# One ring of three PSUM banks for the first MoE's groups and the value products

## The chip, the cores and the metric

The kernel runs on one core of a Trainium2 chip. The core has TensorE (PE) for matmuls, VectorE (DVE), ScalarE (ACT) and GpSimd (POOL) for the rest, and a queue (SP) that here issues nearly all DMAs. A matmul writes into PSUM, of which the kernel has eight banks; ACT and DVE read a product out of its bank, and only then may the next product be written there. The metric is the device time of one execution in microseconds.

## The reference

Attention over 4 batches, 8 heads, 576 tokens and head width 64 with rotary positions, then two MoE-like layers over the 2304 tokens:

```python
q_rot, k_rot = (rotate(q), rotate(k))
scores = scale * np.matmul(q_rot, k_rot.transpose(0, 1, 3, 2))
attn = np.exp(scores - np.max(scores, axis=-1, keepdims=True))
attn = attn / (np.sum(attn, axis=-1, keepdims=True) + 1e-09)
x = np.matmul(attn, v)            # (tokens, 512) after the heads are joined
h = np.maximum(np.maximum(x @ w1, x @ w2), x @ w3)      # first MoE, 512 -> 768
x = h @ w_out                                           # 768 -> 512
h = x @ w_in                                            # second MoE, 512 -> 2048
out = (h * (1.0 / (1.0 + np.exp(-h)))) @ w_out          # 2048 -> 512
```

## The kernel before

Attention runs over 80 tiles. A tile is 128 rows (or 64) of one pair of heads in one batch. For each tile PE computes the scores (L430 to L440, into `s`, of which there is one buffer of three banks), DVE takes the row maximum (L450), ACT takes the exponentials of both heads (L457) and scales them (L469), and four DMAs move blocks of the result from `e` to `pt` (L508), where DVE transposes them (L530). When the two or three tiles of a part are there, `av` (L559) computes the value product into the bank `xp`: one matmul at L571, eight at L575, then a read by ACT (L578) and a second one by DVE (L579), which give the high and the low half of x.

The first MoE of the batches that are done is worked off between the tiles. Its unit is a group (`group`, L662): 12 matmuls for one of the three products of `up` (L680), or 18 for `down` (L708), each of 256 or 320 columns. Of an `up` triple ACT copies the first product out (L687) and DVE takes the running maximum with the second and with the third (L689), so the third can be read only after the second. Of `down` ACT scales the product into `y` (L713), which has two buffers, and a DMA on SP's queue stores it (L714).

`attention` is a generator that yields once for each tile; the loop behind it then takes as many groups as the tile's budget allows. From tile 26 on (`LOOSE`) `b_now[0]` is 1, and a tile's scores are issued behind the last group; the flag goes back to 0 when attention ends. The order that the code is written in is not the order in which the engines work: a scheduler orders each engine's instructions anew from the dependencies and its own estimate of times. Each engine then works strictly in that order.

During attention the eight banks are: three for `s`, two for `tr` (transposes), two for `m` (`ps_m`, the groups) and one for `xp` (`ps_x`, the value products). A `Ring` gives out its buffers in turn, in the order in which the code asks. Tiles are named here as in the built program, by the bank's tag and a running number: `m_4866` and `xp_4866` are the same product in a bank of `m` and in the bank of `xp`.

Of the kernel before, what the change touches and what calls it, by code (L numbers as in the profile page):

```python
# [7 lines left out]
F32 = mybir.dt.float32  # L8
# [9 lines left out]
P = 128  # L18
# [4 lines left out]
def fused_kernel(  # L23
# [52 lines left out]
    ps_m = Ring(ctx, "ps_m", 2, space=PSUM)  # L76
# [20 lines left out]
    ps_x = Ring(attn_pools, "ps_x", 1, space=PSUM)  # L97
# [12 lines left out]
    zscr = {nm: dram.tile([P, KC * (F2 // 512) * 512], F32, name="z" + nm) for nm in ("wi", "wo")}  # L110


    ps_am, b_now = [], [0]

    def max_bank():
        ring, tag = (ps_am[0], "m") if ps_am else (ps_t, "tr") if b_now[0] else (ps_m, "m")
# [256 lines left out]
    def moved(b):  # L373
        return b > 0
# [114 lines left out]
    def blocks(pt):  # L489

        w = pt.shape[2]
        f = pt.rearrange("p c w -> p (c w)")
        return f[:, 0:8 * w].rearrange("p (i c k) -> p i c k", c=8, k=32), f[:, 8 * w:9 * w]
# [65 lines left out]
    def av(b, hp, r):  # L559
        if hp == 0 and r == 0:  # L560
            x_t[b] = x_p[b % 2].tile([P, NP * S], F32, tag="x", name="x").bitcast(F16).rearrange("p (a x s) -> p a x s", a=NP, x=2)
        pt, vv = pt_t.pop((b, hp, r)), v_t[b, hp]
        o, n = PARTS[r][:2]
        v4 = vv[:, 0:4, :].rearrange("p a x -> p (a x)").rearrange("p (h c d) -> p h c d", h=2, c=4)
        xp = ps_x.tile([P, 512], F32, tag="xp", name="xp")
        if moved(b):
            main, mixed = blocks(pt)
            turned = lambda c, g: main[:, :, c + 4 * g, :]
        else:
            mixed, turned = pt[:, 4, :], lambda c, g: pt[:, c + 5 * g, :]  # L570
        nc.tensor.matmul(xp[:, 0:n], vv[:, 4, :], mixed, start=True, stop=False)  # L571
        for c in range(4):
            for g in range(2):
                r = slice(64 * g, 64 * g + 64)
                nc.tensor.matmul(xp[r, 0:n], v4[:, g, c, :], turned(c, g), start=False, stop=(c == 3))  # L575
        xh, xl = x_t[b][:, hp, 0, o:o + n], x_t[b][:, hp, 1, o:o + n]
        sv = sv_t[b][0]
        nc.scalar.activation(out=xh, in_=xp[:, 0:n], func=AF.Copy, scale=sv)  # L578
        nc.vector.scalar_tensor_tensor(  # L579
            out=xl, in0=xp[:, 0:n], scalar=sv, in1=xh, op0=ALU.mult, op1=ALU.subtract  # L580
        )
# [43 lines left out]
    def attention():  # L625

        back = lambda j, n: tiles[j - n] if n <= j < len(tiles) + n else None
        for j in range(len(tiles) + 5):
            b_now[0] = int(j > LOOSE)
            if j < len(tiles):  # L630
                with tc.issue_after(last["group"]) if j > LOOSE else nullcontext():
                    tile_scores(tiles[j])
                tile_max(tiles[j])
            for n in (3, 2):
                key = back(j, n)
                if key and moved(key[0]) and n == 3 - (key in LAST):
                    tile_flip(key)
            for a in av_at.pop(j, ()):
                av(*a)
            key = back(j, 1)  # L640
            if key:
                tile_norm(key)
                if moved(key[0]):
                    tile_move(key)
            key = back(j, 2)
            if key:
                (tile_last if moved(key[0]) else tile_turn)(key)
            for f, a in events.pop(j, ()):
                f(*a)
            yield  # L650
# [11 lines left out]
    def group(passes, n, ps=None, more=False):  # L662

        first = ps is None
        if first:
            wide_n[0] += 1
            ring, tag = (ps_g[0], "mg") if ps_g and wide_n[0] % 7 > 1 else (ps_m, "m")
            ps = ring.tile([P, 512], F32, tag=tag, name=tag)
        for i, (l, r) in enumerate(passes):
            x = nc.tensor.matmul(ps[:, 0:n], l, r, start=(first and i == 0), stop=(not more and i == len(passes) - 1))  # L670
        last["group"] = x.ins
        return ps

    def moe1(b, pools):
# [5 lines left out]
        def up(half, f):  # L680
            o, n = PARTS[half][:2]
            part = []

            def evac(e, ps):
                t = tmp_p.tile([P, n], F32, tag="t", name="t")
                if e == 0:
                    last["ma"] = nc.scalar.activation(out=t, in_=ps[:, 0:n], func=AF.Copy, scale=2.0 ** -22).ins  # L687
                else:
                    last["mv"] = nc.vector.scalar_tensor_tensor(  # L689
                        out=t, in0=ps[:, 0:n], scalar=2.0 ** -22, in1=part[-1], op0=ALU.mult, op1=ALU.max  # L690
                    ).ins
                part.append(t)
                if e == 2:
                    hh = h1[half, f] = h1_p.tile([P, 2, n], F16, tag="h1", name="h1")
                    nc.scalar.activation(out=hh[:, 0], in_=t, func=AF.Copy)
                    nc.vector.tensor_tensor(out=hh[:, 1], in0=t, in1=hh[:, 0], op=ALU.subtract)

            for e in range(3):
                passes = []
                for c in range(KC):  # L700
                    i, fo = (f // FG * KC2 + c // 2) * 3 + e, (c % 2 * FG + f % FG) * P
                    wh, wl = W1.h(i)[:, fo:fo + P], W1.l(i)[:, fo:fo + P]
                    passes += [(wh, x[:, c, 0, o:o + n]), (wh, x[:, c, 1, o:o + n]), (wl, x[:, c, 0, o:o + n])]
                yield half, n * len(passes), False
                ps = group(passes, n)
                evac(e, ps)

        def down(half):  # L708
            o, n = PARTS[half][:2]

            def evac(m, ps):
                ysb = pools[2].tile([P, n], F32, tag="y", name="y")
                last["ma"] = nc.scalar.activation(out=ysb, in_=ps[:, 0:n], func=AF.Copy, scale=cy_t[b]).ins  # L713
                nc.sync.dma_start(out=yscr[:, m, b * S + o:b * S + o + n], in_=ysb)  # L714

            open_ = []
            for m in range(KC):
                passes = []
                for f in range(NF1):
                    wh = WO1.h(f)[:, m * P:(m + 1) * P]  # L720
                    wl = WO1.l(f)[:, m * P:(m + 1) * P]
                    h = h1[half, f]
                    passes += [(wh, h[:, 0]), (wh, h[:, 1]), (wl, h[:, 0])]
                yield half, n * len(passes), True
                if ps_g and half:
                    k = len(passes) - 3
                    open_.append((m, passes[k:], group(passes[:k], n, more=True)))
                else:
                    evac(m, group(passes, n))
            for m, passes, ps in open_:  # L730
                evac(m, group(passes, n, ps))
# [573 lines left out]
    def moe_groups():  # L1305
# [9 lines left out]
    costs = {av: 5800, qk_turn: 2900}  # L1315
    pace = [13600 - 3650 - sum(costs[f] for f, _ in jobs) for jobs in (
        [(av, a) for a in av_at.get(j, ())] + [x for x in events.get(j, ()) if x[0] is qk_turn] for j in range(len(tiles) + 5)
    )]
    debt = 0
# [126 lines left out]
```

## Time and profile before

| | |
|---|---|
| three timed runs | 977.44, 971.39 and 971.1 us, median 971.39 |
| profiled execution | 973.05 us, of it 971.3 us span |
| PE busy | 902.0 us (93%) |
| DVE, ACT, POOL busy | 710.9 (73%), 603.9 (62%), 442.3 us (46%) |
| mean granted TensorE clock | 0.978 |

The span reaches from the first to the last instruction of the profiled execution. Busy shares are means over stages with different limits; the change works only while `b_now[0]` is 1, which is from about 200 to 550 us of the span.

### The profile page before, as it was taken

What the parts mean: (1) busy time and instruction counts of PE and PEld (TensorE: products, weight loads), DVE (VectorE), ACT (ScalarE), POOL (GpSimd) and SP (SyncE); (2) the same over time, 40 slices, a digit from 0 to 9 for tenths busy, and PEclk for the clock granted to TensorE, in tenths of its full rate; (3) what the DMA queues carried; (4) which work ended last, traced back from release to release, by engine and by line L of the source; (5) the groups of instructions that cost most, each with busy time, mean ns of one, the idle gap of its engine ahead of it and who ended that gap; (6) DMA issues with size and microseconds to landing.
All of it is one profiled execution on the core that took longest, in us unless ns stands there. A gap on an engine that the chain in (4) does not pass through costs nothing.

```text
span 971.3 us, 19058 instructions
## 1 busy us (share of the span) xinstructions
PE 902.0 (93%) x6802; PEld 667.4 (69%) x6802; DVE 710.9 (73%) x1295; ACT 603.9 (62%) x1381; POOL 442.3 (46%) x482
## 2 busy tenths in 40 slices
PE   2787898899999899999998999999998999999997
PEld 1454665566655566566654687788887888888886
DVE  6779888867789576898887667465787866856654
ACT  1987587757687666798877535363555545544442
POOL 6745584960325400421211047264486467365363
PEclk9788999999999999999999999999999999999999
DMA  6943034958888984899989763164553434324101
GB/s 153 295 135 108 17 109 125 185 108 187 196 184 192 202 153 87 229 237 244 264 234 208 175 206 126 51 210 130 162 167 99 134 122 136 123 91 136 61 1 44
DMA packets 185198, 146.29 MB, mean 151 GB/s; under 512 B 51216, under 2 KB 168720, under 8 KB 185104
## 3 DMA queue, kind: packets, MB, share of 16 engines
q1 hardware_dynamic: 183600, 144.36, 57.9%
q8 instruction: 54, 0.88, 0.4%
q10 hardware_dynamic: 1504, 0.72, 0.3%
q14 instruction: 40, 0.33, 0.1%
HBM read 90.51 MB, written 26.21 MB: 120 GB/s over the span
## 4 chain that ended last, share of the span: by engine, by line
PE 54%; DMA 10%; DVE 7%; ACT 6%; SPq 4%; issue 3%; POOL 2%; DVEq 0%; ACTq 0%; POOLq 0%
PE m L670 11%; PE m L1102 8%; PE mb L1102 6%; DMA pt<-e 4%; PE c L1165 4%; PE a L1165 4%; PE b L1165 4%; PE xp L575 3%; PE mg L670 3%; PE s L440 3%; ACT e L457 2%; PE d L1165 2%; SPq L508 2%; DMA w8s<-w8scr 2%; POOL gsum L1049 1%
## 5 line engine op out<-in xcount | busy, mean ns | idle before, releaser
L670 PEld LDWEIGHTS <-w 128*128 128x128 f16 x1632 | 160.3, 99 | 62.2 <-issue 18.1
L670 PE MATMUL m<-x,w 128*128 128x256 f16 (+1 forms) x1356 | 188.6, 289 | 10.7 <-DVE t L689 5.1
L1165 PEld LDWEIGHTS <-g 128*128 128x128 f16 x1485 | 145.2, 98 | 16.9
L1102 PEld LDWEIGHTS <-w8s 128*128 128x128 f16 x1344 | 131.0, 98 | 16.1 <-issue 0.9
L450 DVE TENSOR_REDUCE nb<-s 128x2 f32<-128x1152 f32 (+1 forms) x80 | 98.5, 1232 | 37.2 <-PE s L440 30.0
L457 ACT ACTIVATE e<-s,nb 128x576 f32<-128x576 f32 x144 | 105.1, 734 | 28.6 <-DVE nb L450 26.1
L469 ACT ACTIVATE e<-e,rec 128x576 f32<-128x576 f32 x144 | 104.0, 766 | 11.2 <-DVE rec L467 10.4
L366 POOL TENSOR_TENSOR w<-qk,sin_sb 128x512 f32<-128x512 f32 (+2 forms) x40 | 42.8, 1072 | 122.7 <-DMA qk<-in_q_dram 93.5
L575 PE MATMUL xp<-pt,vd 128*64 128x256 f32 (+1 forms) x512 | 79.0, 422 | 0.9 <-DVE pt L530 0.9
L440 PE MATMUL s<-T 64*128 64x512 f32 x256 | 78.7, 685 | 0.0
L970 POOL TENSOR_TENSOR zs<-za 128x128 f32<-128x128 f32 x32 | 16.5, 527 | 129.8 <-DMA za<-zwi 68.3
L530 DVE STREAM_TRANSPOSE pt<-pt 128x1024 f32<-128x1024 f32 (+1 forms) x60 | 67.6, 1127 | 9.4 <-DMA pt<-e 9.4
L1054 DVE SCALAR_TENSOR_TENSOR g<-gsum,sg,g 128x1024 f16<-128x1024 f32 x36 | 49.5, 1383 | 23.7 <-ACT g L1053 23.4
L1116 POOL TENSOR_TENSOR z<-t 128x256 f32<-128x256 f32 x32 | 27.1, 845 | 87.4 <-DVE t L1108 51.3
L1053 ACT ACTIVATE g<-gsum,sg 128x1024 f16<-128x1024 f32 x36 | 40.8, 1141 | 36.4 <-POOL gsum L1049 36.4
L670 PE MATMUL m<-h,wo 128*128 128x256 f16 (+1 forms) x448 | 62.1, 286 | 0.5 <-POOL wo L175 0.3
L575 PEld LDWEIGHTS xp<-pt,vd 128*64 128x64 f32 x512 | 35.6, 139 | 36.7 <-issue 15.7
L670 PEld LDWEIGHTS <-wo 128*128 128x128 f16 x512 | 49.5, 98 | 16.2 <-issue 2.5
L940 POOL TENSOR_TENSOR z<-z 128x256 f32<-128x256 f32 x32 | 29.6, 952 | 41.7 <-DMA z<-zwo 41.2
L1165 PE MATMUL b<-w,g 128*128 128x256 f16 x376 | 48.5, 273 | 0.0
L1165 PE MATMUL a<-w,g 128*128 128x256 f16 x376 | 47.9, 273 | 0.0
L1165 PE MATMUL c<-w,g 128*128 128x256 f16 x376 | 47.6, 273 | 0.0
(265 smaller groups left out, 1989.9 us busy)
## 6 DMA issues: line engine op xcount, KB each, us to landing
w8s<-w8scr SPq DMA_DIRECT2D x64, 448.0 KB, 4.2
pt<-e SPq DMA_DIRECT2D x192, 128.0 KB, 4.0
z<-in_moe_w_in_dram SPq DMA_DIRECT2D x32, 256.0 KB, 3.6
z<-in_moe_w_out_dram SPq DMA_DIRECT2D x32, 256.0 KB, 3.8
w8scr<-w8o SPq DMA_DIRECT2D x32, 256.0 KB, 3.7
w<-in_moe_w_dram SPq DMA_DIRECT2D x6, 768.0 KB, 5.2
wo<-in_moe_w_dram SPq DMA_DIRECT2D x6, 768.0 KB, 5.3
qk<-in_q_dram SPq DMA_DIRECT2D x32, 128.0 KB, 3.1
```

The lines of the kernel that those rows point to most:

```text
L366: tt(out=w4, in0=t4, in1=sin2, op=ALU.mult)
L440: last["s"] = last["score"] = nc.tensor.matmul(s[:, o:o + 512], qs[r], kt[r], start=True, stop=True).ins
L450: x = nc.vector.tensor_reduce(out=nb[:, 0:m], in_=both(s, 0, 960, 576) if m > 1 else s[:, 0:576], op=ALU.max, axis=AX.X, negate=True)
L457: x = nc.scalar.activation(out=e[:, HK[g]], in_=s[:, SK[g]], func=AF.Exp, bias=nb[:, g:g + 1], accum_out=sm[:, g:g + 1])
L469: nc.scalar.activation(out=e[:, HK[g]], in_=e[:, HK[g]], func=AF.Copy, scale=r[:, g:g + 1])
L530: nc.vector.transpose(out=x, in_=x)
L575: nc.tensor.matmul(xp[r, 0:n], v4[:, g, c, :], turned(c, g), start=False, stop=(c == 3))
L670: x = nc.tensor.matmul(ps[:, 0:n], l, r, start=(first and i == 0), stop=(not more and i == len(passes) - 1))
L1053: nc.scalar.activation(out=h, in_=x, func=AF.Copy, scale=sg_t[jb])
L1054: nc.vector.scalar_tensor_tensor(out=l, in0=x, scalar=sg_t[jb], in1=h, op0=ALU.mult, op1=ALU.subtract)
L1102: nc.tensor.matmul(o, l, r, start=(i == 0), stop=(i == len(passes) - 1))
L1165: x = nc.tensor.matmul(ps, l, r, start=first, stop=last_, skip_group_check=True)
```

## The change

A new helper, `product_bank`, counts the products. Two of three get the next buffer of `ps_m`, the third gets the buffer of `ps_x`. While `b_now[0]` is set, both the groups and the value products ask it for their bank; outside that stretch everything is as before. The number of banks, of matmuls, of reads and of DMAs stays the same.

```diff
-    ps_am, b_now = [], [0]
+    ps_am, b_now, third = [], [0], [0]
+
+    def product_bank():
+
+        third[0] += 1
+        ring, tag = (ps_m, "m") if third[0] % 3 else (ps_x, "xp")
+        return ring.tile([P, 512], F32, tag=tag, name=tag)
...
-        xp = ps_x.tile([P, 512], F32, tag="xp", name="xp")
+        xp = product_bank() if b_now[0] else ps_x.tile([P, 512], F32, tag="xp", name="xp")
...
-            ps = ring.tile([P, 512], F32, tag=tag, name=tag)
+            ps = product_bank() if b_now[0] else ring.tile([P, 512], F32, tag=tag, name=tag)
```

The scheduler makes another order of it. In the changed kernel lines from L119 on stand six further down, so that L670 is L676 there. The first place is on PE, between the scores of two neighbouring tiles, `s_4695` and `s_4783`. `4866`, `4960` and `5027` are groups of 12 matmuls of 256 columns, `tr` are transposes. Before:

```order
L440 MATMUL s_4695<-T_3480 128x512 x2
L475 MATMUL tr_4716<-ident_81,e_4529 128x128
L476 MATMUL tr_4716<-ident_81,e_4529 64x128
...
L670 MATMUL m_4960<-x_3716,w_0_141 128x256
...
L670 MATMUL m_5027<-x_3716,w1f_140 128x256
...
L430 MATMUL s_4783<-T_3480,qd_0_124 128x512
L431 MATMUL s_4783<-T_3480,qd_0_124 128x64
L519 MATMUL tr_4801<-ident_81,e_4639 128x128
```

Two whole groups, 24 matmuls, stood between the scores, and `4866` came ahead of them. At the same place of the changed kernel:

```order
L446 MATMUL s_4695<-T_3480 128x512 x2
L481 MATMUL tr_4716<-ident_81,e_4529 128x128
L482 MATMUL tr_4716<-ident_81,e_4529 64x128
...
L676 MATMUL xp_4866<-x_3716,w1f_140 128x256
...
L436 MATMUL s_4783<-T_3480,qd_0_124 128x512
L437 MATMUL s_4783<-T_3480,qd_0_124 128x64
L525 MATMUL tr_4801<-ident_81,e_4639 128x128
...
L676 MATMUL xp_4960<-x_3716,w_0_141 128x256
```

One group, `4866`, now stands between the scores, and `4960`, which takes the same bank, follows behind the second of them; `5027` comes later still.

The second place is SP's queue behind the four moves of `e_3549`. `y_3702` is the output of a `down` group on its way to memory; `pt<-e` are a tile's moves, `z`, `zwi` and `za` weights of the second MoE, `qk` and `vd` inputs. Before:

```order
L508 DMA pt_3571<-e_3549 32x8x128 x4
L854 DMA z_3_3757<-in_moe_w_in_dram 128x256
L829 DMA zwi_137<-z_3595 128x2x128
L308 DMA qk_4166<-in_q_dram 64x2x64
L305 DMA qk_4166<-in_k_dram 128x4x64
L508 DMA pt_3734<-e_3605 32x8x128 x3
L714 DMA yscr_135<-y_3702 128x256
```

Seven DMAs stood between those moves and the store. In the changed kernel:

```order
L514 DMA pt_3571<-e_3549 32x8x128 x4
L321 DMA vd_0_130<-in_v_dram 128x2x256
L970 DMA za_4338<-zwi_137 128x2x128
L720 DMA yscr_135<-y_3702 128x256
L860 DMA z_3_3757<-in_moe_w_in_dram 128x256
```

The store has moved up: two DMAs are now between them.

## Rows read from the trace of the kernel before

**Rows 1.** The page, engines: busy us, share of the span, instructions.

```profile
PE 902.0 (93%) x6802; PEld 667.4 (69%) x6802; DVE 710.9 (73%) x1295; ACT 603.9 (62%) x1381; POOL 442.3 (46%) x482
```

**Rows 2.** Windows: stretch, its length, busy time of each engine, PEclk, DMA share, GB/s.

```profile
200.00:550.00 350.00, 334.02 (x2219) 213.06 (x2216) 278.53 (x557) 266.68 (x739) 89.17 (x120) 0.99 0.86 195
```

**Rows 3.** PE's waits from 200 to 550 us: total us, times, longest us.

```profile
PE m L670 <- DVE t L689: 4.3, 3, 2.4
PE s L437 <- ACT e L457: 3.6, 6, 0.9
PE m L670 <- ACT y L713: 2.1, 1, 2.1
PE s L430 <- ACT e L457: 1.9, 3, 1.2
PE m L670 <- ACT t L687: 1.5, 1, 1.5
```

**Rows 4.** Timeline of PE: start us, us, instruction, [idle before <-releaser].

```profile
268.21 0.38 PE L670 MATMUL m<-x,w1f 128*128 128x256 f16 x2 [0.63 <-DVE t L689]
...
317.27 1.79 PE L670 MATMUL m<-x,w 128*128 128x320 f16 x12 [1.49 <-ACT t L687]
334.48 0.43 PE L670 MATMUL m<-x,w1f 128*128 128x320 f16 x2 [2.06 <-ACT y L713]
...
425.25 1.47 PE L670 MATMUL m<-x,w 128*128 128x256 f16 x12 [1.29 <-DVE t L689]
...
516.72 4.97 PE L670 MATMUL m<-x,w 128*128 128x320 f16 x24 [2.41 <-DVE t L689]
```

**Rows 5.** Timeline of ACT and DVE, the reads that those matmuls waited for.

```profile
316.78 0.44 ACT L687 ACTIVATE t<-m 128x320 f32<-128x320 f32 x1
...
333.95 0.47 ACT L713 ACTIVATE y<-m,cy 128x256 f32<-128x256 f32 x1 [3.35 <-DMA yscr<-y]
...
424.80 0.40 DVE L689 SCALAR_TENSOR_TENSOR t<-m,t 128x256 f32<-128x256 f32 x1
...
515.04 1.25 DVE L530 STREAM_TRANSPOSE pt<-pt 128x1024 f32<-128x1024 f32 x1 [3.36 <-DMA pt<-e]
516.21 0.45 DVE L689 SCALAR_TENSOR_TENSOR t<-m,t 128x320 f32<-128x320 f32 x1
```

**Rows 6.** Timeline of SP's queue around the store of y.

```profile
322.21 2.69 SPq L508 DMA_DIRECT2D pt<-e  x4
...
329.65 0.55 SPq L714 DMA_DIRECT2D yscr<-y  x1
```

**Rows 7.** Timeline, one tile's scores, its maximum, its second exponential, the next scores.

```profile
408.43 1.13 PE L440 MATMUL s<-T 64*128 64x512 f32 x4
...
409.75 1.34 DVE L450 TENSOR_REDUCE nb<-s 128x2 f32<-128x1152 f32 x1
...
412.04 0.72 ACT L457 ACTIVATE e<-s,nb 128x576 f32<-128x576 f32 x1
...
412.91 1.12 PE L430 MATMUL s<-T,qd 128*128 128x512 f32 x2 [0.36 <-ACT e L457]
```

**Rows 8.** Timeline, the end of `4866` (5 of these 17), its read by ACT.

```profile
405.90 2.02 PE L670 MATMUL m<-x,w 128*128 128x256 f16 x17
...
408.78 0.38 ACT L687 ACTIVATE t<-m 128x256 f32<-128x256 f32 x1
```

**Rows 9.** Windows behind two of the waits; PEclk is the third number from the end.

```profile
335.00:339.00 4.00, 4.00 (x22) 2.12 (x21) 0.17 (x1) 3.88 (x12) 3.76 (x4) 0.57 0.95 195
...
516.00:520.00 4.00, 3.28 (x13) 1.84 (x13) 3.87 (x10) 3.30 (x9) 0.00 (x0) 0.57 0.55 176
```

**Rows 10.** Groups of DVE, 200 to 550 us, and timeline of one value product.

```profile
L579 DVE SCALAR_TENSOR_TENSOR x<-xp,vs,x 128x256 f16<-128x256 f32 (+1 forms) x22 | 11.2, 510 | 12.0 <-ACT x L578 11.8
...
404.76 0.76 PE L575 MATMUL xp<-pt,vd 128*64 128x320 f32 x4
...
408.55 0.55 DVE L579 SCALAR_TENSOR_TENSOR x<-xp,vs,x 128x320 f16<-128x320 f32 x1
```

## The prediction

> **What bounds the kernel now.** I began with the page: PE is busy 93% of the span and no other engine over 73% [rows 1], so PE bounds it, and a change that adds no matmul can only give or take PE's idle time and its slow stretches. The table by stretches then narrows this to the only part that the change touches: from 200 to 550 us PE is busy 334.0 of 350 us [rows 2], so 16.0 us is idle there. PE's own waits in that stretch say for what [rows 3]. A product waits for a bank to be read out: 4.3 behind DVE, 2.1 and 1.5 behind ACT, together 7.9 us in five waits. The scores wait for the one score buffer: 3.6 + 1.9 = 5.5 us in nine waits. The rest is small. The timeline shows the five bank waits one by one: 0.63, 1.49, 2.06, 1.29 and 2.41 us [rows 4].
>
> Two of them cost more than their idle time. In the 4 us behind the waits of 2.06 and 2.41 us the granted clock is 0.57 on the mean [rows 9], so most of that time is at the lower of the two levels, 1.2 GHz instead of 2.4. What this costs is seen at 516.72: 24 matmuls took 4.97 us [rows 4]; at the pace of 317.27, where 12 took 1.79 us and so one follows the other after (1.79 - 0.30)/11 = 0.135 us, they would take 23 x 0.135 + 0.30 = 3.41. That is 1.5 us, and I take the same for the other stretch. All that the banks cost is 7.9 + 3.0 = 10.9 us, and this bounds what more freedom in banks can give.
>
> **Why those waits arise** decides what a third bank does for them [rows 5]. At 334.48 ACT's read began only at 333.95, because ACT had stood 3.35 us for a store of y. At 516.72 DVE's read began at 516.21, behind a transposition that had itself waited 3.36 us for its moves. At 425.25 the read at 424.80 was that of the third product of a triple that PE had worked ahead of the second; it had to wait for the second's maximum. Only at 317.27 had PE simply come too soon: 12 matmuls' end to the read at 316.78 is ordinary. So four of five come from a reader that is late, not from a bank that is asked for too often.
>
> **The change part by part.** It adds no instruction. A group's bank is now asked for again three products later, but the value products count among the three, and their bank is no longer their own. So I counted, for each product on PE's new order, the matmuls between the last of the bank's former holder and its own first, at 0.135 us for 320 columns and (2.02 - 0.27)/16 = 0.109 us for 256 [rows 4, 8].
>
> *The five waits.* At 317.27 the former holder is now a value product that is long done: -1.5, the whole. At 425.25 the predecessor is the second of its triple and no longer the third, which passes its bank to a later group: -1.3. At 268.21 the predecessor is the same, with 4.9 us of work between where there were 4.2: -0.6, the whole. At 516.72 it is also the same, with 4.3 us in place of 3.4: -0.9, and 1.5 us stay, with their slow stretch, as long as the transposition waits for its moves as it did. At 334.48 predecessor and work between are as before (4.0 us), so the third bank itself gives nothing. But the store of y that ACT waits for has moved up in SP's queue. Before, SP ended the four moves at 322.21 + 2.69 = 324.90 and came to the store at 329.65 [rows 6], seven DMAs and 4.75 us later, 0.68 us each. Now two stand between, 1.4 us, so that the store goes 3.4 us earlier and covers the 3.35 us: -2.1 and -1.5 for the clock. If one of those two DMAs waits for its buffer, this is 0. Together -7.9, between -1.5 (317.27 alone) and -10.9.
>
> *The scores.* From the end of one tile's scores to the next there must be time for the maximum and both exponentials: the scores that began at 408.43 ended at 409.56, the second exponential at 412.76, and PE went on at 412.91 [rows 7], so about 3.4 us. PE hides that with what stands in between. At this place that was 24 matmuls and two transposes, 2.9 us, and PE waited 0.36. Now 12 matmuls stand there, 12 x 0.109 + 0.3 = 1.6 us: the wait becomes 1.8. Over all 54 pairs of neighbouring tiles, before, 11 had less than 3.4 us between them and lacked 5.6 us in sum, where 5.5 was measured as the nine waits [rows 3]; now 15 have less and lack 10.7. I take the difference, +5.1, behind which stands the tile's whole chain. Ends: 0, if these waits fall into the same gaps as others, and +7, with one slow stretch more.
>
> *Other returns of a bank.* Six are now under 2.1 us of work, before two were in this stretch. The shortest is `4866` to `4960`: only one score and one transpose, 1.1 us, stand between. ACT read `4866` until 409.16, after it had ended at 405.90 + 4 x 0.109 + 0.27 = 406.6 [rows 8], 2.6 us; but the wait of 1.8 us for `s_4783` stands between the two, so it costs nearly nothing more. The other five have 1.6 to 2.1 us. I take +1.5 for all of them, between 0 and +6 (one microsecond each), near the low end since the one return that I could time is hidden.
>
> The waits of transposes for new q and k, and those of value products for their moved blocks, I leave at nothing: they hang on POOL and the DMAs, and PE works the value products later than before, not earlier.
>
> **Sum.** -7.9 + 5.1 + 1.5 = -1.3 us. The profiled execution of 973.05 would become 971.8; it lies 1.7 above the median of 971.39, from which I get **970.1 us**.
>
> **A rule against this count.** The five waits have shown a reader that is late [rows 5], and two banks that already turn. The Trainium skill, Perfetto Trace Analysis, in Matmuls under Optimizing Tensor Performance, says that independent groups should rotate through different banks so that the reading of one overlaps the next one's matmuls. By that rule one bank more in the turn takes all five waits away; the trace agrees with it at 317.27 alone. That is the first rival.
>
> **The rivals.** *Faster: the third bank covers all bank waits*, and the scores find their cover as before. For it: 7.9 us of 16.0 idle us are bank waits [rows 2, 3], and half of all products now have over 4.3 us between. Against it: the late readers and the thinner cover of the scores. It gives -10.9, 960.5 us. Chance 0.2.
>
> *Slower: the value product holds up the ring.* A value product is read twice, by ACT and then by DVE. The example ended at 404.76 + 0.76 = 405.52 and was free when DVE had done, at 409.10 [rows 10], 3.6 us later. Before, only the next value product, many microseconds later, needed that bank; now a group does, with 3.7 us of work between on the median and about 3 in the tenth part with the least. There are 22 such products in the stretch [rows 10]. While the second read comes within 3.6 us this costs nothing; it decides as soon as DVE comes later than 3.7. With half a microsecond for each, 22 x 0.5 = 11.0, and one more slow stretch of 1.5: 970.1 + 12.5 = 982.6 us. For it: DVE waited 11.8 us for ACT's half of that read [rows 10], and DVE has a maximum, a transposition and weights in its queue. Against it: most of these reads came sooner. Chance 0.22.
>
> *The banks were not what counted*: the waits go and come back elsewhere, 971.4. That lies inside the forecast, not beside it.
>
> **How the numbers follow.** A measurement of this kernel can tell about 1% from no change, 9.7 us. The forecast, within 1%, has 0.58; the faster rival 0.2, the slower one 0.22, and these are also the chances of the three outcomes. The least sum is -10.9 + 0 + 0, the greatest -1.5 + 7 + 6 = +11.5, so 960.5 to 982.9. Each rival sits at one of these ends with a fifth, and about half of each lies beyond: I take 960 to 983.
>
> **What would show it.** In the changed trace from 200 to 550 us: PE's bank waits some 3 us and no more than 5; none at 317, and the one behind the store of y gone, with the store close behind the four moves and a clock of 1.0 there; the scores' waits about 10 us, one of some 1.8 us ahead of `s_4783`. Idle time of PE near 15 us, and one slow stretch in place of two. I am wrong if the scheduler's new order makes a long wait that this count cannot see, since it takes the readers' delays as they were: a queue of DVE or ACT that now stands at another DMA moves a bank's return by 3 us and brings a slow stretch along.

## The result

The changed kernel takes 980.61 us (median of 10 runs, 977.09 to 985.47), the kernel before 975.06 us in the 10 runs beside it (969.34 to 978.0). The ratio is 1.0064 with an interval of 1.0040 to 1.0088. So the change costs 0.64%. That lies inside the forecast range, but the forecast was a small gain, and no change at all is ruled out by the interval. The profiled execution took 980.79 us (span 978.7 us), 7.7 us more than the profiled one before.

### The profile after

On the page PE does the same work as before [rows 1]: 902.3 us in 6802 matmuls. What has grown is the rest of the span.

```profile
PE 902.3 (92%) x6802; PEld 667.4 (68%) x6802; DVE 712.0 (73%) x1295; ACT 604.5 (62%) x1381; POOL 442.7 (45%) x482
```

The windows of the changed kernel say where: PE's idle time from 200 to 550 us rose from 16.0 us [rows 2] to 23.6. The last two rows are the 4 us behind the waits at 334 and 518 (PEclk third from the end).

```profile
200.00:550.00 350.00, 326.38 (x2169) 207.48 (x2167) 276.34 (x548) 262.85 (x729) 91.71 (x122) 0.99 0.87 192
...
334.50:338.50 4.00, 4.00 (x23) 2.15 (x23) 0.54 (x2) 4.00 (x13) 1.56 (x4) 0.64 1.09 245
...
518.00:522.00 4.00, 2.20 (x15) 1.36 (x14) 3.92 (x9) 3.62 (x11) 0.00 (x0) 1.00 0.51 131
```

PE's waits of the changed kernel from 200 to 560 us, in the columns of [rows 3]: the scores now wait 8.2 + 4.0 = 12.2 us (before 5.5), and the products wait for a bank 4.2 + 3.2 + 2.5 + 0.6 = 10.5 us (before 7.9). So in this profile the wait that the third bank was to shorten is longer, and the other has more than doubled. A second profile of each kernel, further down, has 8.5 us of bank waits for 9.3, and 12.6 us of scores' waits for 6.4: that the scores wait twice as long repeats, that the banks' waits rose does not.

```profile
PE s L436 <- ACT e L463: 8.2, 7, 2.0
PE m L676 <- ACT y L719: 4.2, 1, 4.2
PE s L443 <- ACT e L463: 4.0, 6, 1.3
PE m L676 <- DVE t L695: 3.2, 2, 2.3
PE xp L676 <- DVE x L585: 2.5, 2, 2.2
...
PE xp L577 <- DVE t L695: 0.6, 1, 0.6
```

The timeline of PE in the changed kernel shows the waits that answer to [rows 4], and the largest new ones. Those of 317 and 425 us are gone. The one at 334 is twice as long as before, the one at 518 is 0.88 us. Those at 540 and 553, and the scores' wait at 394, were not there. 414.63 is `s_4783`.

```profile
333.96 0.69 PE L676 MATMUL m<-x,w1f 128*128 128x320 f16 x2 [4.18 <-ACT y L719]
...
393.81 1.12 PE L436 MATMUL s<-T,qd 128*128 128x512 f32 x2 [2.02 <-ACT e L463]
...
414.63 1.13 PE L436 MATMUL s<-T,qd 128*128 128x512 f32 x2 [1.37 <-ACT e L463]
...
518.23 2.20 PE L676 MATMUL m<-x,w 128*128 128x320 f16 x15 [0.88 <-DVE t L695]
...
540.50 0.43 PE L676 MATMUL m<-h,wo1f 128*128 128x320 f16 x2 [2.27 <-DVE t L695]
...
552.89 0.43 PE L676 MATMUL xp<-h,wo1f 128*128 128x320 f16 x2 [2.20 <-DVE x L585]
```

The timeline of ACT and DVE shows the readers behind three of them, as [rows 5] did before. ACT was free at 326.51 and stood until the store of y had ended. At 540 and 553 DVE had stood at a transposition whose moves had not come, and read the product only afterwards. At 540 only 1 us of other work lies between the two. At 553 there is more: ACT stood 1.72 us for the store of a weight and came to its half of the read at 550.40, and DVE did 3 us of other work between the transposition and its own half. Behind the longest wait of the scores, at 394, stands a late maximum: DVE began it at 390.82, though those scores had ended at 387.84.

```profile
326.32 0.19 ACT L472 ACTIVATE rec<-sm 128x2 f32<-128x2 f32 x1
333.44 0.48 ACT L719 ACTIVATE y<-m,cy 128x256 f32<-128x256 f32 x1 [6.93 <-DMA yscr<-y]
...
390.82 1.35 DVE L456 TENSOR_REDUCE nb<-s 128x2 f32<-128x1152 f32 x1
...
537.71 1.25 DVE L536 STREAM_TRANSPOSE pt<-pt 128x1024 f32<-128x1024 f32 x1 [3.37 <-DMA pt<-e]
...
539.98 0.47 DVE L695 SCALAR_TENSOR_TENSOR t<-m,t 128x320 f32<-128x320 f32 x1
...
547.90 1.25 DVE L536 STREAM_TRANSPOSE pt<-pt 128x1024 f32<-128x1024 f32 x1 [2.45 <-DMA pt<-e]
549.67 0.72 ACT L950 ACTIVATE w8o<-zs,wihalf 128x512 f16<-128x512 f32 x1 [1.72 <-DMA w8scr<-w8o]
...
552.30 0.53 DVE L585 SCALAR_TENSOR_TENSOR x<-xp,vs,x 128x320 f16<-128x320 f32 x1
```

And SP's queue in the changed kernel, to be held against [rows 6]: only two DMAs stand between the moves and the store, as forecast, but the moves themselves have sunk from 322.21 to 325.65, and the store is issued at 329.64 as it was at 329.65. Between these moves and the four moves of the tile ahead of them, which start at 315.53 (314.71 before, second block), now stand ten DMAs in place of six.

```profile
315.53 3.86 SPq L514 DMA_DIRECT2D pt<-e  x4
...
325.65 2.69 SPq L514 DMA_DIRECT2D pt<-e  x4
328.39 0.61 SPq L321 DMA_DIRECT2D vd<-in_v_dram  x1
329.05 0.49 SPq L970 DMA_DIRECT2D za<-zwi  x1
329.64 0.41 SPq L720 DMA_DIRECT2D yscr<-y  x1
```

```profile
314.71 2.74 SPq L508 DMA_DIRECT2D pt<-e  x4
```

### The profile page after: what moved, and what is told of

Same layout as the page of the kernel before. It is cut to its first block, busy times and chain, and to the rows that moved or that the text cites. A ratio compares the mean times of both kernels' runs of the same rounds, so it can differ in the third digit from the quotient of the medians.

```text
span 978.7 us, 19036 instructions
## 1 busy us (share of the span) xinstructions
PE 902.3 (92%) x6802; PEld 667.4 (68%) x6802; DVE 712.0 (73%) x1295; ACT 604.5 (62%) x1381; POOL 442.7 (45%) x482
## 4 chain that ended last, share of the span: by engine, by line
PE 56%; DVE 10%; DMA 7%; ACT 5%; issue 3%; SPq 2%; POOL 2%; DVEq 0%; ACTq 0%; POOLq 0%
PE m L676 9%; PE m L1108 8%; PE mb L1108 6%; PE c L1171 4%; PE a L1171 4%; PE b L1171 4%; PE s L446 3%; DMA pt<-e 3%; PE mg L676 3%; PE xp L676 3%; PE d L1171 2%; PE xp L581 2%; PE m L581 2%; SPq L514 2%; DVE pt L536 2%
## 5 line engine op out<-in xcount | busy, mean ns | idle before, releaser
L676 PEld LDWEIGHTS <-w 128*128 128x128 f16 x1632 | 159.3, 99 | 59.6 <-issue 15.7
L676 PE MATMUL m<-x,w 128*128 128x256 f16 (+1 forms) x1040 | 146.3, 288 | 7.6 <-ACT t L693 3.1
L1122 POOL TENSOR_TENSOR z<-t 128x256 f32<-128x256 f32 x32 | 27.1, 847 | 88.8 <-DVE t L1114 53.9
L676 PEld LDWEIGHTS <-wo 128*128 128x128 f16 x512 | 49.5, 98 | 17.6 <-issue 3.8
L676 PE MATMUL m<-h,wo 128*128 128x256 f16 (+1 forms) x368 | 51.7, 286 | 0.8 <-DVE h L702 0.3
L581 PE MATMUL xp<-pt,vd 128*64 128x320 f32 (+1 forms) x320 | 47.3, 414 | 1.2 <-DVE pt L536 1.2
L373 POOL TENSOR_TENSOR qk<-qk,cos_sb 128x512 f32<-128x512 f32 (+2 forms) x44 | 46.3, 1056 | 2.8
```

The lines of the kernel that those rows point to most:

```text
L373: tt(out=t4, in0=t4, in1=cos2, op=ALU.mult)
```

## The experiments

In time order, in groups. Ratios are to the kernel before, run beside each. The quoted texts name theories by letters; what a letter stands for is said with each group.

**Which part of the stretch.** Theory A: the loss is made in the last tiles of attention, where the new waits of 2.27 and 2.20 us stand. Theory B: it is made earlier, by the new order. `shared[0]` takes the place of `b_now[0]` in the two calls of `product_bank`, and is set for a part of the tiles:

```diff
+            shared[0] = int(LOOSE < j < 75)
```

> The ring of three works only from tile 26 to 74; from tile 75 on groups and value products have their own banks again. PE's order is that of the changed kernel up to about 508 us. Theory A (the loss is made in the last tiles, where a down group waits for the third product of a triple and another for the second read of a value product, 2.3 and 2.2 us, and two scores for 0.8 and 0.7 us): the loss of 5 to 6 us goes, ratio to the kernel before 1.000, 0.997 to 1.003. Theory B (the loss is spread: the scores' thinner cover costs 6.7 us all over the stretch): 1.004 to 1.007, as the whole change.

Measured: 978.01 against 974.01 us, ratio 1.0038 (1.0019 to 1.0057).

The second has the ring only in the last tiles:

```diff
+            shared[0] = int(j >= 75)
```

> The complement: the ring of three only from tile 75 to the end of attention, own banks before. PE's order is that of the kernel before up to about 525 us. Theory A: nearly the whole loss, 4 to 7 us, ratio 1.004 to 1.007, with waits of over 2 us for a bank between 530 and 560 us. Theory B: at most a tenth of the stretch, so under 1 us, ratio 0.999 to 1.001.

Measured: 974.69 us, ratio 1.0017 (0.9994 to 1.0041); no bank wait above 2 us stands from 530 to 560 us. Theory A falls as the main cause: by the medians more than half of the loss is there without the last tiles. Theory B's figures are missed too: 1.0038 lies a little below its 1.004 to 1.007, and 1.0017 above its 0.999 to 1.001, so a part of the loss does belong to the last tiles.

**The value products keep their own bank**, and the groups take three in turn all the same, so that `xp` serves both in an order of its own:

```diff
-        xp = product_bank() if b_now[0] else ps_x.tile([P, 512], F32, tag="xp", name="xp")
+        xp = ps_x.tile([P, 512], F32, tag="xp", name="xp")
```

> Value products always take the bank xp; the groups alone take three banks in turn, so that every third group shares xp with the value products. Theory A: groups that wait for DVE's second read of a value product, and value products behind groups, stay, so no gain on the change: ratio 1.002 to 1.010. Theory B: the ring's length is what thins the scores' cover; with value products out of the count the order comes nearer to that of before: 0.999 to 1.004.

Measured: 995.82 us, ratio 1.0211 (1.0180 to 1.0242), far beyond what either theory gave. PE's waits from 190 to 575 us are those of groups for that one bank, 18.7 us in the three largest lines:

```profile
PE xp L676 <- DVE x L585: 8.8, 6, 3.8
PE xp L676 <- DVE t L695: 5.1, 2, 3.1
PE xp L676 <- ACT t L693: 4.8, 2, 4.4
```

The first line, 8.8 us, is the prediction's slower rival: a group waits for the second read of a value product. In the other two, 9.9 us, the group waits for the reads of another group in that bank. The changed kernel, where the value product takes its turn, keeps most of this away: 2.5 us behind L585.

**The store of y.** Theory C: the wait behind the store of y makes the loss. The store is issued by ACT, in the changed kernel and in the kernel before:

```diff
-                nc.sync.dma_start(out=yscr[:, m, b * S + o:b * S + o + n], in_=ysb)
+                nc.scalar.dma_start(out=yscr[:, m, b * S + o:b * S + o + n], in_=ysb)
```

> The changed kernel with the stores of y issued by ACT and not by SP. PE's order of groups and scores is nearly the changed kernel's: 15 pairs of scores with too little work between them, 10.7 us lacking, as there. Theory C (the 4.2 us wait at 334 us and its slow stretch come from SP's queue, which is issuing without a pause and comes to the store of y 7 us after ACT has written it): ACT's wait of 6.9 us for that store falls under 2 us, PE's wait behind L719 goes, -4 to -6 us against the changed kernel, ratio to the kernel before 0.999 to 1.003. Theory D (the store goes out late for the DMAs in flight, whoever issues it): the wait stays at 3 to 5 us, ratio 1.005 to 1.010, ACT's issuing coming on top.

Measured: 985.66 against 973.81 us, ratio 1.0121 (1.0091 to 1.0150). PE's wait behind the read into y is gone, but another stands in its place. The timeline of this kernel: ACT stood 7.96 us, and the instruction that it stood at is the store itself. Its data were written at 321.57, but it was issued at 328.97, just after a load of k had landed at 328.89. In the trace the issue of the store waits for the semaphore that this load raises (a counter that tells when a DMA has landed). ACT's next instruction follows at 329.62, and PE stood 5.48 us behind ACT.

```profile
328.97 0.33 ACTq L720 DMA_DIRECT2D yscr<-y  x1
329.62 1.44 ACT L475 ACTIVATE e<-e,rec 128x576 f32<-128x576 f32 x2 [7.96 <-DMA qk<-in_k_dram]
...
332.52 1.22 PE L577 MATMUL xp<-pt,vd 128*128 128x256 f32 x2 [5.48 <-ACT pt L526]
```

> The same edit on the kernel before, with two banks for the groups and one for the value products. Theory C: the wait of 2.1 us behind the store of y at 334 us and its slow stretch go, ratio 0.995 to 0.998. Theory D: 0.999 to 1.003. The difference to the run above is the ring of three with this one late reader out of the way: by theory B, that thinner cover of the scores is the bulk of the loss, it stays 4 to 6 us; if the late reader was the bulk, it falls to 1 to 2 us.

Measured: 971.48 us, ratio 0.9983 (0.9964 to 1.0002). So with the same store the ring of three costs 1.4%, not less than without. Theory C falls as it was put. What the store's wait itself costs stays open, since this edit moved the wait and did not take it away, in this kernel too: ACT stood 6.73 us ahead of the same store, issued at 331.23.

**The order held fast.** Each group's matmuls are issued behind the scores last written, in both kernels:

```diff
+        with tc.issue_after(last["score"]) if b_now[0] else nullcontext():
             for i, (l, r) in enumerate(passes):
                 x = nc.tensor.matmul(ps[:, 0:n], l, r, ...)
```

> The kernel before, but each group's matmuls are ordered behind the scores issued last, so that scores and groups stand on PE as the code issues them, and the scheduler cannot move a group across a tile's scores. Counted on the order: 16 pairs of scores with too little work between, 21.3 us lacking (before 5.6), returns of a bank as before or somewhat shorter. Theory B: 12 to 18 us slower than before, ratio 1.012 to 1.019, PE's waits of scores for ACT at 15 to 21 us. If the scores' cover does not decide: 1.000 to 1.004.

Measured: 987.58 against 973.81 us, ratio 1.0155 (1.0124 to 1.0186).

> The changed kernel with the same ordering. Counted on the order: 7 pairs of scores lack 13.2 us, and no return of a bank has less than 2.7 us of work, the median 5.3 (4.4 in the changed kernel). Theory B: scores wait some 13 us, banks under 4 us, ratio to the kernel before 1.002 to 1.009, and so 5 to 12 us faster than the run above: with the order held, three banks in one ring do help. If the ring itself is at fault, whatever the order (a group waits for the value product's second read), it is no faster than the run above.

Measured: 983.43 us, ratio 1.0104 (1.0065 to 1.0142), a little above the expected interval. With the groups tied to the scores, no cost of the third bank is seen: the changed kernel is not slower than the other, rather some 4 us faster, though the intervals overlap. The two orders are still not the same one, as the counts in the expectations show. What costs in both is the scores: 8.8 + 7.6 + 6.2 = 22.6 us in e6_pin_before, 10.4 + 5.5 + 5.3 = 21.2 in e7_pin_after, with 1.5 and 3.4 us of bank waits. The profile puts some of these waits down to a weight's operation on DVE (L254, 10.4 us; L248 in the kernel before, 7.6 us), but in each of those three of e7_pin_after the second exponential ended within 0.1 us of PE's start. PE's waits in e7_pin_after, 200 to 560 us:

```profile
PE s L443 <- DVE z L254: 10.4, 3, 4.7
PE s L436 <- ACT e L463: 5.5, 5, 1.8
PE s L443 <- ACT e L463: 5.3, 8, 2.5
PE xp L677 <- DVE x L585: 1.4, 1, 1.4
PE m L677 <- ACT t L694: 1.1, 1, 1.1
PE m L677 <- DVE x L585: 0.9, 1, 0.9
```

**The groups in order.** Of the groups, 12 `up` triples of the stretch are worked out of order in the changed kernel, 2 before. Here each group is only held behind the group before it:

```diff
+        with tc.issue_after(last["group"]) if b_now[0] and "group" in last else nullcontext():
```

> The changed kernel, with each group's matmuls issued behind the group before it, so that no triple of the first MoE is worked out of order; the value products and the scores stay free. Counted on PE's order, the scores lack 13.9 us of cover (changed kernel 10.7), and two returns of a bank are under 2.1 us of work (six). Theory O (triples worked out of order make the readers late, and that is what the ring of three costs): from 190 to 575 us the bank waits fall from some 10 us to 4.5 or less, and the ratio to the kernel before is 1.000 to 1.004. Theory S (the scores' cover decides): the scores' waits rise from 12 to 14 to 17 us, the ratio is 1.006 to 1.010.

Measured: 981.08 against 974.42 us, ratio 1.0079 (1.0051 to 1.0107). Groups wait 8.1 us, but 4.2 of these are two waits of `down` groups for their input h (L703), not for a bank. That leaves 3.9 us for a bank, 4.7 with a value product that waits for one, where the changed kernel has 10.5; the scores wait 10.7 us. So the bank waits fell about as theory O said, and the time did not follow, so theory O falls by the time. Theory S gave the time, but its scores' waits of 14 to 17 us did not come, and what holds this kernel at +0.79% is only in part named by its waits.

> The kernel before, with each group's matmuls issued behind the group before it. Counted: the scores lack 8.2 us (before 5.6), one return under 2.1 us (three). Theory O: the wait of 1.3 us behind the third product of a triple goes, the rest stays, ratio 0.998 to 1.002. Theory S: scores' waits 8 us in place of 5.5, ratio 1.001 to 1.004.

Measured: 976.10 us, ratio 1.0025 (1.0003 to 1.0048). This one weighs the two waits against each other: PE's waits from 200 to 560 us show 4.0 us for banks in place of 7.9, the scores 10.6 in place of 5.5 [rows 3], and the kernel is no faster for it.

```profile
PE s L437 <- ACT e L457: 6.1, 8, 2.0
PE s L430 <- ACT e L457: 4.5, 5, 2.2
PE m L671 <- DVE t L690: 3.0, 3, 2.2
...
PE m L671 <- ACT y L714: 0.4, 1, 0.4
PE m L671 <- ACT t L688: 0.3, 1, 0.3
PE m L671 <- ACT x L578: 0.3, 1, 0.3
```

**Both kernels once more**, unchanged, for a second profile of each.

> The changed kernel once more, for a second profile. If what was read from the first is no accident of one execution: scores' waits 11 to 13 us from 200 to 560 us, bank waits 9 to 12 us, among them one of some 4 us at 334 behind the read into y, and those at 540 and 553 behind DVE.

Measured: 980.88 us, one run. Scores' waits 7.9 + 4.7 = 12.6 us; bank waits 4.0 + 2.5 + 2.0 = 8.5, a little under the expected 9: the one behind the read into y was 1.96 us, not 4.2; those at the end stand as before.

> The kernel before once more, for a second profile. Scores' waits 5 to 6.5 us, bank waits 7 to 9 us in the same five places.

Measured: 975.11 us, one run. Scores' waits 6.4 us, bank waits 9.3 in five waits with the same releasers, 0.3 above the expected end.

The wait behind the store of y in this second pair: ACT's read into y stood 5.06 us in the changed kernel (first block) and 3.60 us in the kernel before (second block).

```profile
330.25 0.47 ACT L719 ACTIVATE y<-m,cy 128x256 f32<-128x256 f32 x1 [5.06 <-DMA yscr<-y]
```

```profile
338.85 0.47 ACT L713 ACTIVATE y<-m,cy 128x256 f32<-128x256 f32 x1 [3.60 <-DMA yscr<-y]
```

PE's wait behind it was 1.96 us (2.71 before), and the granted clock in the 4 us behind it 1.00 in both.

**The stretch cut in three.** Between the same scores the profiles of a kernel can be laid side by side. I took the scores `s_2602`, `s_3781` and `s_4896`, which start at 239.92, 328.75 and 418.97 us before. In PE's timeline of the changed kernel they are:

```profile
239.84 0.38 PE L443 MATMUL s<-kd,T 128*128 128x128 f32 x2
...
326.12 0.38 PE L443 MATMUL s<-kd,T 128*128 128x128 f32 x2
...
421.00 0.49 PE L443 MATMUL s<-kd,T 128*128 128x128 f32 x2
```

So the changed kernel is 2.6 us quicker from the first to the second (86.28 for 88.83 us) and 4.7 us slower from there to the third (94.88 for 90.22). Theory L: gain and loss lie in different thirds. Rival U: every turn of the ring costs alike. The edit is that of e1_early with other tiles:

```diff
+            shared[0] = int(LOOSE < j < 48)
```

> The ring of three only in the first third of its stretch, up to tile 47 (some 330 us); then groups on two banks and value products on their own, as before. PE's order is the changed kernel's up to there and that of before from there on; counted, the scores lack 4.5 us of cover over all pairs (before 5.6, changed kernel 10.7). Theory L (the third bank helps where the new order keeps the scores covered; in both profiles of the changed kernel the scores at 329 us start some 4 us earlier than before, reckoned from those at 173): some of that gain stays, ratio 0.995 to 0.999, bank waits from 190 to 575 us 4 to 7 us, scores' waits 4 to 6. Rival U (the loss is spread over every turn of the ring, some 6 us over 54 tiles): a third of it, ratio 1.001 to 1.004.

Measured: 971.64 against 975.02 us, ratio **0.9962 (0.9941 to 0.9984)**: faster than both kernels. PE's waits of this kernel from 330 to 515 us: the scores 1.6 + 0.7 = 2.3 us, as before, and the wait behind the store is there with 3.7 us all the same.

```profile
PE m L677 <- ACT y L720: 3.7, 1, 3.7
PE m L677 <- DVE t L696: 2.7, 2, 1.4
PE s L436 <- ACT e L463: 1.6, 2, 1.2
...
PE s L443 <- ACT e L463: 0.7, 2, 0.4
```

The other kernel has the ring in the middle tiles instead:

```diff
+            shared[0] = int(47 < j < 75)
```

> The complement: the ring of three only from tile 48 to tile 74 (some 330 to 515 us). PE's order is that of before up to 330 us, then the changed kernel's up to 515; counted, the scores lack 11.5 us of cover. Theory L: all of the loss without the gain ahead of it, ratio 1.005 to 1.010, scores' waits 11 to 13 us. Rival U: half of the loss, ratio 1.002 to 1.004.

Measured: 981.87 us, ratio 1.0069 (1.0048 to 1.0090). The same view of this kernel: the scores 4.7 + 3.0 = 7.7 us, line for line what the changed kernel has from 330 to 515.

```profile
PE s L436 <- ACT e L463: 4.7, 3, 2.0
PE m L677 <- ACT y L720: 2.7, 1, 2.7
PE s L443 <- ACT e L463: 3.0, 4, 1.3
```

Both results are where theory L put them and outside what rival U allows. The table gives the profiles of all kernels that share an order, from their starts of those scores and their spans. Where the ring works in the middle, 36 group matmuls of 256 columns stand behind the third mark that stood ahead of it, and six of the eight matmuls of a value product ahead that stood behind: 36 x 0.109 - 6/8 x 2.38 = 2.1 us. "Corrected" adds these to the second stretch and takes them from the third.

| kernel | ring in tiles | 1st to 2nd mark | 2nd to 3rd, corrected | 3rd to end, corrected | scores' waits 200-330, 330-515 | group waits 200-330, 330-515, 515-565 |
|---|---|---|---|---|---|---|
| before, two profiles | none | 88.8, 89.4 | 90.2, 89.4 | 552.3, 551.1 | 2.6, 2.2; 2.9, 2.3 | 2.1, 3.4, 2.4; 2.2, 3.9, 3.2 |
| after, two profiles | all | 86.3, 86.3 | 97.0, 95.2 | 555.6, 558.8 | 2.1, 7.7; 2.5, 7.7 | 0, 4.5, 5.7; 0, 2.3, 6.5 |
| e1_early | to 74 | 87.3 | 95.6 | 552.6 | 2.0, 7.8 | 0, 2.9, 3.0 |
| e2_late | from 75 | 89.2 | 88.6 | 555.6 | 2.9, 2.3 | 2.1, 3.5, 3.3 |
| e12_first | to 47 | 85.3 | 91.7 | 550.4 | 2.0, 2.3 | 0, 6.4, 0 |
| e13_middle | 48 to 74 | 89.1 | 96.6 | 554.1 | 2.8, 7.7 | 2.1, 3.0, 4.6 |

The columns of the first two stretches fall into two classes by where the ring works. Against the two profiles of before it gains 1.5 to 4 us in the first stretch, and all group waits go there; a value product's wait of 0.6 us for a group's bank is new in two of the four profiles. In the second it costs 5 to 8, and the scores' waits rise by 5.5, in the same seven waits to 0.1 us in all four profiles. The group waits are no larger there on the whole; 0.3 us of them are for the input h and not for a bank. From the third mark on the changed kernel loses 3 to 8 us more, which e1_early undoes almost wholly. Not all the profiled executions lie at their medians: that of e12_first is 3.7 us faster, those of e13_middle and e2_late 3.7 and 4.7 us slower.

## Why the prediction was wrong

The sum has the wrong sign. Of the 10.5 us between the forecast of 970.1 and the measured 980.61, 3.7 are not the change's: the median of the three runs that the forecast stood on was 971.39, that of ten is 975.06. The other 6.9 are the sum's. Its terms against what was measured, in the profiled executions; the last column is the second pair:

| term | forecast | measured | e10_again_after less e11_again_before |
|---|---|---|---|
| 317.27, with no reader late | -1.5 | -1.5 | -1.6 |
| 425.25 | -1.3 | -1.3 | -1.2 |
| 268.21 | -0.6 | 0: 0.61 us now ahead of a value product, at L577 | -0.6 |
| 516.72 | -0.9, slow stretch stays | -1.5, and -1.5 for the clock, 1.00 now | -1.4, clock 1.00 in both |
| 334.48, the store of y | -2.1 and -1.5 for the clock | +2.1, clock 0.64 | -0.7, clock 1.00 in both |
| scores | +5.1 | +6.7 | +6.2 |
| other returns of a bank | +1.5 | +4.8 (0.3, 2.27, 2.20) | +4.8 (0.35, 2.29, 2.17), clock 0.66 behind the last |
| sum | -1.3 | +7.8 (profiled executions: 7.7) | +5.5 without the clock (profiled executions: 5.8) |

**The step that failed** is the one on the store: "so that the store goes 3.4 us earlier and covers the 3.35 us: -2.1 and -1.5 for the clock". It counted the DMAs between the moves and the store, and took the moves to stay where they were. Seven had become two, but ten in place of six stand ahead of the moves, and SP issues there with pauses of some 0.1 us at most. From the start of the moves ahead to the store it is 14.9 us before and 14.1 in the changed kernel (15.3 and 14.0 in the second pair): 0.8 to 1.3 us won, not 3.4. ACT meanwhile came to its read 4.1 us earlier (326.51 for 330.60), and 5.4 us in the second pair, counted from the first mark. So ACT's wait for the store, forecast to go, grew in both pairs, from 3.35 to 6.93 and from 3.60 to 5.06 us. PE's wait behind it, 2.06 and 2.71 us before, is 4.18 and 1.96 us in the two profiles of the changed kernel, 2.6 in e1_early and 3.7 in e12_first: nowhere gone, though not shown to be longer. This step accounts for 5.7 of the 9.1 us between the two sums in the first pair and for 2.9 of 6.8 in the second. The next largest, and steadier, is "other returns of a bank", sized at +1.5 us and measured at +4.8 in both pairs. That the first pair's sum meets the whole to 0.1 us is in part luck, for it leaves out a slow stretch near 750 us, which comes up below.

**The clock.** The slow stretches were priced from one profile, as if each went with its wait. In the second profile of the kernel before, the waits at the same two places are longer, 2.71 and 3.17 us, and the granted clock behind them is 1.00. So the 3.0 us of clock in the bound and the 1.5 in the sum are no steady part of those waits, and the -1.5 measured at 516.72 is not shown to be the change's.

**Mis-sized in the right direction.** The scores' term holds: 12.2 us where 5.5 + 5.1 = 10.6 were forecast, and `s_4783` waits 1.37 us where 1.8 were forecast and 0.36 was before. There the cover is what fails: PE went on 3.05 us after the last scores had ended (411.58 to 414.63), no later than the 3.35 us of before, and had 12 matmuls to fill it in place of 24. The count could not see most of the 2.02 us at 394, since there DVE's maximum was late as well. That an order alone can bring such waits is shown by e9_order_before, which has 10.6 us of them without the ring; e12_first and e13_middle show that the ring brings them in one part of the tiles and not in another. The changed kernel's own order without the ring was not run. "Other returns" was taken near its low end because the one that I could time was hidden. The two that cost 2.27 and 2.20 us are those where DVE had stood at a transposition, at 553 together with ACT's wait for another store. This is what the prediction named as its own undoing, readers' delays that do not stay as they were, but it gave it no price.

**The rivals.** The faster rival, that a third bank takes the bank waits away, is right up to 330 us and wrong behind it. The rule of the Trainium skill (Perfetto Trace Analysis, Matmuls) that independent groups should rotate through different banks agrees with the trace there: group waits fall from 2.1 us to 0 in all three kernels with the ring in those tiles. The slower rival, the value product that holds up the ring, was 2.5 us and not 11; with a bank fixed to it, in e5_own_bank, it was 8.8.

**Open.** What the last tiles lose is seen (5.7 and 6.5 us of group waits for 2.4 and 3.2) but no run separates the late moves of DVE's transpositions from the ring there: e13_middle, whose ring has ended by then, has 4.6 us of them too. From 700 to 800 us the granted clock is 0.98 in both profiles of the changed kernel and 1.00 in both of the kernel before. The slow stretch lies behind a wait of 2.65 us that both kernels have (752.63 and 746.84). It is not the ring's doing: e9_order_before has 0.98 without the ring, e8_order_after 1.00 with it. What decides it is open, and so is how much of the 3 to 8 us behind the third mark it makes.

## What to carry to other kernels

A buffer more helps where the reader is on time; where it is late, look for what holds the reader. When an order is made anew from the change, compare the whole queue up to the point in question, not the distance between two neighbours in it, and price the cover that the next critical operation loses. And a change that is a small loss over its whole stretch can be a gain in a part: lay profiles side by side between the same instructions, and cut there. Take two profiles of each kernel before a term is named: here a second pair turned the sign of one and took the clock out of two.

## Not expected of the hardware

Two profiles of one kernel can repeat better between marks than in absolute time: the first mark of the kernel before came at 239.92 and at 243.55 us, while from there to the second it took 88.83 and 89.44; the changed kernel took 86.28 us in both. From the second mark to the third its two profiles differ by 1.7 us. The seven waits of the scores from 330 to 515 us repeat one by one to 0.01 us in the two profiles of the changed kernel and in e13_middle. A store moved from SP's queue to ACT's can hold ACT itself: that of e3_store_act was issued 7.4 us after its data, when a load of k had landed whose semaphore its issue waits for, and ACT stood 7.96 us. How long PE waited does not say whether the clock falls behind the wait: 2.06 and 2.41 us were followed by 0.57 for 4 us [rows 9], 2.71 and 3.17 us at the same places of e11_again_before by 1.00, and the wait of 2.65 us near 750 us by 1.00 before and by 0.77 to 0.88 in the changed kernel.
